# Channel attention over 384 x 384 x 384 in two passes: the opening of the second pass re-cut, two packed blocks stored together, 24-row reads up to then

## The chip, the cores and the metric

One core of a Trainium2 chip runs the whole kernel in one launch. The metric is the time of one execution on the device in microseconds (us), less is better. An execution can also be recorded by the hardware profiler; its page and its trace are what is read here. In a page PE is TensorE (matrix products), DVE VectorE, ACT ScalarE, POOL GpSimd and SP SyncE, which here only issues loads. "SPq" and "ACTq" are those engines' instruction queues, from which transfers (DMAs) are issued: loads from SP, stores from ACT.

## What is computed

```python
def reference(x, w1, w2):                 # x: 1 x 384 x 384 x 384, w1: 384 x 96, w2: 96 x 384, all bf16
    xf = x.reshape(B, H * W, C)
    gap = jnp.mean(xf, 1)                 # mean over all pixels, per channel
    gmp = jnp.amax(xf, 1)                 # maximum over all pixels, per channel
    h_a = gap @ w1
    h_a = h_a * (h_a > 0)
    h_m = gmp @ w1
    h_m = h_m * (h_m > 0)
    scale = sigmoid(h_a @ w2 + h_m @ w2)
    return x * scale[:, None, None, :]
```

The scale depends on every pixel, so `x` (113 MB) is read once for the mean and the maximum, and each element is multiplied and written after that. What doesn't stay on the chip in between has to be read a second time.

## The kernel before

The 147,456 pixels are cut into 1,152 rows for each of the 128 partitions. "A row" below is one pixel of 384 channels in every partition, 128 x 768 bytes = 98,304 bytes; a load of n rows moves n x 768 contiguous bytes for each partition.

**First pass.** SP loads blocks of rows; TensorE sums them (L260), VectorE keeps a running maximum in `acc`, 11 rows wide (L326). What can stay on the chip stays: 96 rows at the start of the buffer `body` (three slots of 31, 31 and 34 rows, at `body` rows 0, 31 and 62), 21 rows in `held`, 10 rows in PSUM, and seven packed blocks. A packed block is 32 rows in the space of 24 (`homes[i]`, `body` rows 96 + 24 i and on): three parts a, b and w of 8 rows, and a part d of 8 rows whose bytes are hidden in the others by `pack`. If a test finds values that the packing can't hold (`bad`), these blocks are read again at the very end; with this data they are not.

**Between the passes.** The maximum is folded, both branches go through `w1` and `w2`, and the scale lands in `scale_bc` (L418). The first rows of `held` (8, `refill`) and the 11 rows of `acc` are loaded in the meantime from SP (L402, L399).

**Second pass, opening** (L526 to L538). `put` multiplies pieces of a buffer in place on VectorE (L423) and has ACT store each (L432); `put_acc` does the same for `acc`. It begins with the first 6 rows of slot 0, then `acc`, the rest of slot 0, `held`, then slots 1 and 2. In between, `read(-1, 0)` has SP load the first of the rows that are needed again, into rows of `body` whose stores are done: SP waits in its own queue until the stores of just these rows have landed.

**Second pass, turns** (L546 to L564). `PLACES` lists, for each of the 28 turns, the first row of `body` and the number of rows that the turn's read goes to; `RING` = 96 rows, and after some packed stores also `body` rows from 96 up. A turn multiplies its rows on VectorE, has ACT store them (L477), has SP read into every place that is free by then (`read(turn, gone)`, L520), and then does one entry of `jobs`: `unpack(i, h)` restores half h of packed block i (eight instructions on VectorE, L455 and L460, and six copies on ACT, L474), `finish(i)` multiplies a restored block, 24 rows of `homes[i]` and 8 rows of `homes_d[i]`, the place where part d was restored to. Blocks 0 and 1 are also stored by `finish`, as is part d of block 2; the others are stored in the last three turns (`after`). `gone` tells `read` that the rows from 96 up may be used: it is set after turn 3, where block 0 is finished and stored, and place (96, 24) is the ninth. The three last stores (`leaving`) bring rows that were kept in PSUM, by way of `held` and `acc`.

Each engine takes its instructions in the order in which they are written; loads share one queue (q1 in the page) and stores another (q10), both over the same 16 DMA engines.

Of the kernel before, what the change touches and what calls it, by code (L numbers as in the profile page):

```python
# [32 lines left out]
RING = 96  # L33
G = 8
PACKED = 7
PSUM_ROWS = 8
LATE_ROWS = 8
BANK_ROWS = 2
# [14 lines left out]


PLACES = (
    ((0, 24), (24, 24), (48, 24), (72, 24)) * 2 + ((96, 24),)
    + ((0, 30), (30, 30), (60, 30), (90, 30)) * 4 + ((0, 30), (30, 30), (60, 26))
)
FIRST_READ = (8, 8, 8)
FILLS = 16  # L60
FIRST_STORES = ((1, 2, 3, 4, 4, 5, 6, 6), (9, 10, 12), (16, 18))
HELD_STORES = (6, 7)
ACC_STORES_AT = 3
TEST_SCALE = 0.031187
SUM_TAIL = 4
MM_ROWS = 4
# [3 lines left out]
def kernel(  # L70
# [22 lines left out]
    def rows_of(ap, block):  # L93
        first, n = block
        return ap[first * P:(first + n) * P, :].rearrange("(p n) c -> p n c", n=n)
# [8 lines left out]
    def take(n):  # L104
        nonlocal at
        at += n
        return at - n, n

    ps_block = take(PSUM_ROWS)
    beside = take(BANK_ROWS + A)  # L110
    packed_block = take(GP * PACKED)
    held_block = take(sum(LAST_HELD))
    stay = {s: take(sum(pieces)) for s, pieces in STAYING.items()}
# [28 lines left out]
    acc = consts.tile([P, A, C], BF16)  # L142
    nc.dynamic_dma_scratch_size = RING_BYTES
    nc.lookup_mloc("DynamicDMAScratchLoc").dims = [P, RING_BYTES]
    held = nc.alloc_sbuf_tensor_at("held", [P, HELD_ROWS, C], BF16, offset=RING_BYTES).ap()
    body = xpool.tile([P, RING + 3 * G * PACKED, C], BF16, name="body")
    slots = [body[:, SLOT * i:SLOT * i + stay[i][1], :] for i in range(NS)]
    spare = body[:, SLOT * NS, :]
    homes = [body[:, RING + 3 * G * i:RING + 3 * G * (i + 1), :] for i in range(PACKED)]
# [67 lines left out]
    for i in range(PACKED):  # L217
        first, d_at = 3 * G * i, 3 * G * PACKED + G * i
# [20 lines left out]
    for block, buf, pieces in parts_left:  # L239
        for j, m in enumerate(pieces):  # L240
            lo = sum(pieces[:j])
# [86 lines left out]
    def turn_over(out_, rows):  # L328

        for r in range(LATE_ROWS):  # L330
            for q in range(CQ):
                nc.tensor.transpose(  # L332
                    out=out_[:, r, q * P:(q + 1) * P], in_=rows[:, r, q * P:(q + 1) * P], identity=ident_bf
                )
# [11 lines left out]
    for st in steps:  # L346
# [8 lines left out]
        _, block, rows, lo, hi = st  # L355
# [9 lines left out]
        j = max(0, min(m, A - done))  # L365
# [55 lines left out]
    def multiply(dst, src):  # L421
        n = dst.shape[1]
        nc.vector.tensor_tensor(  # L423
            out=dst, in0=src, in1=scale_bc.unsqueeze(1).to_broadcast([P, n, C]), op=ALU.mult
        )

    def put(block, buf, pieces, lo=0):
        j = 0
        for m in pieces:
            rows = buf[:, j:j + m, :]  # L430
            multiply(rows, rows)
            nc.scalar.dma_start(out=rows_of(orr, block)[:, lo + j:lo + j + m, :], in_=rows)  # L432
            j += m

    def put_acc():
        for lo, hi in acc_pieces:
            multiply(acc[:, lo:hi, :], acc[:, lo:hi, :])
            nc.scalar.dma_start(out=acc_rows(orr, lo, hi), in_=acc[:, lo:hi, :])


    turns = len(PLACES)
    homes_d = [held[:, G * (i % 2):G * (i % 2 + 1), :] for i in (1, 0, 1)]
    homes_d += [homes[1][:, G * i:G * (i + 1), :] for i in range(3)] + [held[:, 0:G, :]]
    assert len(homes_d) == PACKED
    HG = G // 2
    m = held[:, 2 * G:2 * G + HG, :]
# [29 lines left out]
    def store(buf, block, lo):  # L476
        nc.scalar.dma_start(out=rows_of(orr, block)[:, lo:lo + buf.shape[1], :], in_=buf)  # L477

    d_at = 3 * G * PACKED

    def finish(i):

        for rows in (homes[i], homes_d[i]):
            multiply(rows, rows)
        if i < 2:
            store(homes[i], packed_block, 3 * G * i)
        if i < 3:
            store(homes_d[i], packed_block, d_at + G * i)


    jobs = [[(unpack, 0, 0)], [(unpack, 0, 1)], [(unpack, 1, 0)], [(finish, 0)], [(unpack, 1, 1)], [], [(finish, 1)]]
    jobs += [[(unpack, 2, 0)], [(unpack, 2, 1)], []]
    for i in range(3, PACKED):
        jobs += [[(unpack, i, 0)], [(finish, i - 1)], [(unpack, i, 1)]]
    jobs.append([])
    jobs.append([(finish, PACKED - 1)])

    after = [
        [(body[:, RING + 3 * G * 2:RING + 3 * G * 4, :], 3 * G * 2)],
        [(body[:, RING + 3 * G * 4:RING + 3 * G * 6, :], 3 * G * 4)],  # L500
        [(homes[1], d_at + 3 * G), (homes_d[6], d_at + 6 * G), (homes[6], 3 * G * 6)],
    ]

    order = []
# [2 lines left out]
    def read(last_turn, blocks_gone):  # L507

        if not again:
            return False  # L510
        k = len(PLACES) - len(again)
        lo, n = PLACES[k]
        if lo + n > RING + 3 * G * blocks_gone or max(turn_of_row[lo:lo + n]) > last_turn:
            return False
        turn_of_row[lo:lo + n] = [k] * n
        buf, b = body[:, lo:lo + n, :], again.pop(0)
        assert b[1] == n
        j = 0
        for m in FIRST_READ if k == 0 else (n,):
            nc.sync.dma_start(out=buf[:, j:j + m, :], in_=rows_of(xr, b)[:, j:j + m, :])  # L520
            j += m
        assert j == n
        order.append((b, buf))
        return True

    k = ACC_STORES_AT  # L526
    put(stay[0], slots[0], FIRST_STORES[0][:k])
    put_acc()
    j = sum(FIRST_STORES[0][:k])
    put(stay[0], slots[0][:, j:, :], FIRST_STORES[0][k:], j)  # L530
    put(held_block, held[:, LATE_ROWS:, :], HELD_STORES, LATE_ROWS)
    put(refill, held[:, 0:LATE_ROWS, :], (LATE_ROWS,))
    read(-1, 0)
    put(stay[1], slots[1], FIRST_STORES[1])
    read(-1, 0)
    put(stay[2], slots[2], FIRST_STORES[2])
    read(-1, 0)
    read(-1, 0)  # L538
    nc.vector.tensor_scalar(out=flag, in0=bad_ps, scalar1=0.5, scalar2=None, op0=ALU.is_gt)
# [1 line left out]
    assert len(jobs) <= turns - 3  # L541
    gone = 0

    leaving = [(held[:, G:G + PSUM_ROWS, :], ps_block), (acc[:, 0:LATE_ROWS, :], held_block)]
    leaving.append((acc[:, LATE_ROWS:LATE_ROWS + BANK_ROWS, :], beside))
    for turn in range(turns):  # L546
        b, buf = order.pop(0)
        multiply(buf, buf)
        if turn >= turns - len(after):
            for rows, lo in after[turn - turns + len(after)]:  # L550
                store(rows, packed_block, lo)
        store(buf, b, 0)
        while read(turn, gone):
            pass
        for job, *which in jobs.pop(0) if jobs else ():
            job(*which)
            gone = gone or job is finish
        if turn == turns - 3:
            to = leaving[1][0]
            nc.vector.tensor_copy(out=to.bitcast(U32), in_=late.bitcast(U32))  # L560
            turn_over(late, to)
            multiply(leaving[0][0], kept_ps[:, 0:PSUM_ROWS, :])
            multiply(leaving[2][0], kept_b)
            multiply(to, late)  # L564
# [40 lines left out]
```

## Time and profile before

| | us |
|---|---|
| three runs: median (lowest to highest) | 729.07 (729.03 to 729.39) |
| the profiled execution, its own time | 729.27 |
| its span in the page | 727.5 |
| VectorE busy | 565.0 (78%) |
| ScalarE busy | 349.5 (48%) |
| TensorE busy | 189.8 (26%) |
| HBM read / written | 192.14 MB / 113.25 MB, 420 GB/s over the span |

The span is what the profiler saw from the first instruction to the last; some 1.8 us of the execution lie around it. The page's second part cuts the span into 40 slices of 18.2 us, with a busy share in tenths for each engine and the bytes moved in each. A window gives the same for any stretch: start and end, length, busy time and number of instructions of PE, PEld (weight loads), DVE, ACT and POOL, the granted clock of TensorE, the share of DMA engines that were busy, and GB/s. A DMA share a little over 1 comes from packets whose records overlap. A line of waits reads "who <- whom: total us, times, longest". The chain of work that ended last is listed as start, duration, what. For a transfer the trace also has the time of its issue and of its landing, when the last of its bytes is told to have arrived, and the time that each packet (one partition's bytes) took.

The first pass ends near 273 us, the opening of the second runs from 278.0 to 305, its first turn starts at 306.6 and its last multiply ends at 680.8; the last store lands at 725.8.

### The profile page before, as it was taken

Reading aid. Unit: us, or ns where it says so; the run is one execution under the profiler, and the core shown is the slowest. Engines: PE = TensorE matmul, PEld = TensorE weight load, DVE = VectorE, ACT = ScalarE, POOL = GpSimd, SP = SyncE. Lnnn points to the kernel's source line nnn. Section 1 sums busy time; section 2 is a strip of 40 time slices with the busy share of each in tenths; the row PEclk is TensorE's granted clock in tenths of the full one; section 3 lists DMA queues with packets and bytes.
Section 4 is the critical chain, followed back from the end, with each engine's and each line's share of the span. In section 5 each row is a group of like instructions: output and inputs, shape, how many; then the busy total and the mean of one; then the engine's idle time right before and its main releaser. Section 6 shows DMA issues by size and latency. Waiting matters only on the chain.

```text
span 727.5 us, 3877 instructions
## 1 busy us (share of the span) xinstructions
PE 189.8 (26%) x1357; PEld 73.9 (10%) x1357; DVE 565.0 (78%) x440; ACT 349.5 (48%) x251; POOL 0.7 (0%) x6
## 2 busy tenths in 40 slices
PE   5767577885657461000000000000000000000000
PEld 1222222232222140000000000000000000000000
DVE  6799999999999998979969372989688894954200
ACT  6979999999999100058042703063443603000000
POOL 0000000000000000000000000000000000000000
PEclk9879877797897555555555555555555555555555
DMA  9999999999999979999999999999999999999997
GB/s 382 430 429 420 434 422 434 432 424 430 428 427 421 421 312 332 424 422 427 436 426 431 434 431 427 434 429 427 432 431 431 436 431 429 437 431 439 430 426 328
DMA packets 22563, 305.63 MB, mean 420 GB/s; under 512 B 2864, under 2 KB 3472, under 8 KB 9616
## 3 DMA queue, kind: packets, MB, share of 16 engines
q1 hardware_dynamic: 14048, 192.14, 62.3%
q10 hardware_dynamic: 8496, 113.25, 36.5%
q8 instruction: 10, 0.16, 0.1%
q14 instruction: 9, 0.07, 0.0%
HBM read 192.14 MB, written 113.25 MB: 420 GB/s over the span
## 4 chain that ended last, share of the span: by engine, by line
DMA 64%; DVE 26%; issue 2%; PE 1%; SPq 0%; ACT 0%; DVEq 0%; ACTq 0%
DMA body<-in_x_dram 47%; DMA out_dram<-body 17%; DVE body L423 13%; DVE acc L326 10%; DVE held L423 1%; PE words_ps L308 1%; DVE held L455 1%; PE bank_a L260 0%; DVE acc L423 0%; DVE acc L460 0%; DVE body L460 0%; DVE kept_ps L380 0%; DVE body L455 0%; DVE acc L455 0%; DVE acc L367 0%
## 5 line engine op out<-in xcount | busy, mean ns | idle before, releaser
L423 DVE TENSOR_TENSOR body<-body,scale_bc 128x11520 bf16<-128x11520 bf16 (+14 forms) x51 | 220.2, 4352 | 90.3 <-DMA body<-in_x_dram 87.5
L326 DVE TENSOR_TENSOR acc<-acc,body 128x2304 bf16<-128x2304 bf16 (+4 forms) x210 | 229.7, 1168 | 14.6 <-DMA body<-in_x_dram 14.5
L260 PE MATMUL bank_a<-body,small 128*1 128x512 bf16 (+2 forms) x849 | 92.2, 477 | 81.9 <-DMA body<-in_x_dram 81.9
L332 PE MATMUL words_ps<-ident_bf,acc 128*128 128x128 bf16 x24 | 2.7, 313 | 375.9 <-DVE acc L560 375.9
L288 ACT ACTIVATE held<-held 128x3072 uint8<-128x3072 uint8 (+1 forms) x35 | 82.1, 2346 | 1.1
L474 ACT COPY body<-body 128x1536 uint8<-128x1536 uint8 x20 | 29.5, 1477 | 93.5 <-DVE body L423 93.1
L287 ACT ACTIVATE held<-body,held 128x3072 uint8<-128x3072 int8 (+1 forms) x28 | 62.0, 2214 | 9.4 <-DMA body<-in_x_dram 9.0
L474 ACT COPY held<-body 128x1536 uint8<-128x1536 uint8 x8 | 11.8, 1476 | 100.8 <-DVE body L423 59.8
L474 ACT COPY body<-acc 128x1536 uint8<-128x1536 uint8 x34 | 49.6, 1475 | 8.0 <-DVE acc L460 7.6
L260 PEld LDWEIGHTS <-small 128*1 128x1 bf16 x891 | 30.4, 96 | 143.7 <-issue 123.2
L332 PEld LDWEIGHTS <-acc 128*128 128x128 bf16 x24 | 2.5, 147 | 376.3 <-DVE acc L560 376.3
L308 PE MATMUL words_ps<-body,scale_bc 128*128 128x512 fp8e4 (+1 forms) x126 | 39.4, 427 | 2.7 <-ACT body L315 2.7
L308 PE MATMUL words_ps<-body,w_sb 128*128 128x512 fp8e3 x84 | 27.2, 408 | 0.0
L308 PE MATMUL words_ps<-held,body 128*128 128x512 fp8e4 x84 | 25.5, 385 | 0.0
L314 ACT COPY body<-held 128x1536 uint8<-128x1536 uint8 x14 | 20.6, 1472 | 0.0
L474 ACT COPY acc<-body 128x1536 uint8<-128x1536 uint8 x14 | 20.5, 1468 | 0.0
L314 ACT COPY body<-body 128x1536 uint8<-128x1536 uint8 x14 | 20.5, 1463 | 0.0
L315 ACT ACTIVATE body<-words_ps 128x1536 uint16<-128x1536 f32 x14 | 20.2, 1442 | 0.0
L287 ACT ACTIVATE held<-held 128x3072 uint8<-128x3072 int8 x7 | 20.0, 2857 | 0.2
L326 DVE TENSOR_TENSOR acc<-acc,held 128x1920 bf16<-128x1920 bf16 (+4 forms) x18 | 17.5, 1012 | 0.1
L308 PE MATMUL words_ps<-body 128*128 128x512 fp8e3 x42 | 16.5, 394 | 0.0
L455 DVE TENSOR_SCALAR held<-held 128x1536 uint16<-128x1536 uint16 x28 | 15.7, 560 | 1.0
(71 smaller groups left out, 169.7 us busy)
## 6 DMA issues: line engine op xcount, KB each, us to landing
body<-in_x_dram SPq DMA_DIRECT2D x20, 2976.0 KB, 21.7
body<-in_x_dram SPq DMA_DIRECT2D x19, 2880.0 KB, 22.1
out_dram<-body ACTq DMA_DIRECT2D x18, 2880.0 KB, 26.2
body<-in_x_dram SPq DMA_DIRECT2D x14, 2304.0 KB, 16.6
out_dram<-body ACTq DMA_DIRECT2D x13, 2304.0 KB, 29.5
out_dram<-body ACTq DMA_DIRECT2D x2, 4608.0 KB, 42.1
held<-in_x_dram SPq DMA_DIRECT2D x8, 768.0 KB, 22.5
body<-in_x_dram SPq DMA_DIRECT2D x5, 960.0 KB, 15.3
```

The source lines that it names most:

```text
L260: nc.tensor.matmul(sum_ps[q * QP:q * QP + 1, 0:g * P], lhsT=ones_bf[:, 0:1], rhs=rows[:, k:k + g, q * P:(q + 1) * P], start=(done + k == 0 ...
L287: nc.scalar.activation(out=out_, in_=rows, func=ACT.Square, bias=test_bias, scale=TEST_SCALE)
L288: nc.scalar.activation(out=out_, in_=out_, func=ACT.Square, bias=minus4, accum_out=tests[:, k:k + 1],)
L308: nc.tensor.matmul(words[:, c:c + BANK], lhsT=weights[2 * r + k], rhs=high(part(i, r), dt)[:, half * n + c:half * n + c + BANK], start=(r ...
L314: nc.scalar.copy(out=high(part(i, r), U8)[:, span], in_=low(part(i, r + 2), U8)[:, span])
L315: nc.scalar.activation(out=part(i, 2).rearrange("p n c -> p (n c)").bitcast(U16)[:, span], in_=words, func=ACT.Copy, bias=32767.5,)
L326: nc.vector.tensor_tensor(out=out_, in0=in0, in1=in1, op=ALU.max)
L332: nc.tensor.transpose(out=out_[:, r, q * P:(q + 1) * P], in_=rows[:, r, q * P:(q + 1) * P], identity=ident_bf)
L423: nc.vector.tensor_tensor(out=dst, in0=src, in1=scale_bc.unsqueeze(1).to_broadcast([P, n, C]), op=ALU.mult)
L455: nc.vector.tensor_scalar(out=u16(dst), in0=u16(src), scalar1=s1, scalar2=s2, op0=op0, op1=op1)
L474: nc.scalar.copy(out=dst, in_=src)
```

## The change

- `PLACES`: three rounds of four places of 24 rows in place of two, then (96, 24), then three rounds of 30 and a last one of 30, 30, 30 and 20 rows: 29 turns and not 28, for the same 782 rows. The first read comes in two pieces (8, 16) and not three.
- The opening starts with the last 7 rows of slot 0 (3, 4), then `acc`, then all of `held`, then the other 24 rows of slot 0 (8 to 16, 16 to 24, 0 to 8). Before the second read come the first 17 rows of slot 1 (8, 9) and the first 10 of slot 2, and then the other 14 and 24 rows in one piece each.
- `finish` stores nothing for block 0. When block 1 is finished (turn 6), blocks 0 and 1 leave in one store of 48 rows and their parts d, now side by side in `held`, in one of 16. Part d of block 2 stays in `held` until the end. `gone` is set with block 1.
- Jobs for blocks 2 to 6 come later in the list; part d of block i is restored to another place (`homes_d`).
- The rows that were kept in PSUM leave by way of `body` rows 110 to 120 and not of `held` and `acc`; `late` still leaves from `acc`.

```diff
 PLACES = (
-    ((0, 24), (24, 24), (48, 24), (72, 24)) * 2 + ((96, 24),)
-    + ((0, 30), (30, 30), (60, 30), (90, 30)) * 4 + ((0, 30), (30, 30), (60, 26))
+    ((0, 24), (24, 24), (48, 24), (72, 24)) * 3 + ((96, 24),)
+    + ((0, 30), (30, 30), (60, 30), (90, 30)) * 3 + ((0, 30), (30, 30), (60, 30), (90, 20))
 )
-FIRST_READ = (8, 8, 8)
+FIRST_READ = (8, 16)
-FIRST_STORES = ((1, 2, 3, 4, 4, 5, 6, 6), (9, 10, 12), (16, 18))
+OPENING = (0, 24, (3, 4))
+FIRST_PLACE = ((0, 8, (8, 8)), (0, 0, (8,)))
+SECOND_PLACE = ((1, 0, (8, 9)), (2, 0, (10,)))
+OTHER_PLACES = ((1, 17, (14,)), (2, 10, (24,)))
...
-    homes_d = [held[:, G * (i % 2):G * (i % 2 + 1), :] for i in (1, 0, 1)]
-    homes_d += [homes[1][:, G * i:G * (i + 1), :] for i in range(3)] + [held[:, 0:G, :]]
+    homes_d = [held[:, G * (i % 2):G * (i % 2 + 1), :] for i in range(4)]
+    homes_d += [homes[1][:, G * i:G * (i + 1), :] for i in range(3)]
...
-        if i < 2:
-            store(homes[i], packed_block, 3 * G * i)
-        if i < 3:
-            store(homes_d[i], packed_block, d_at + G * i)
+        if i == 1:
+            store(body[:, RING:RING + 3 * G * 2, :], packed_block, 0)
+            store(held[:, 0:2 * G, :], packed_block, d_at)
...
-    jobs += [[(unpack, 2, 0)], [(unpack, 2, 1)], []]
+    jobs += [[], [], [], [(unpack, 2, 0)], [(unpack, 2, 1)]]
...
-        [(homes[1], d_at + 3 * G), (homes_d[6], d_at + 6 * G), (homes[6], 3 * G * 6)],
+        [(held[:, 0:2 * G, :], d_at + 2 * G), (homes[1], d_at + 4 * G), (homes[6], 3 * G * 6)],
...
-    k = ACC_STORES_AT
-    put(stay[0], slots[0], FIRST_STORES[0][:k])
+    def put_slot(i, lo, pieces):
+        put(stay[i], slots[i][:, lo:, :], pieces, lo)
+
+    put_slot(*OPENING)
     put_acc()
-    j = sum(FIRST_STORES[0][:k])
-    put(stay[0], slots[0][:, j:, :], FIRST_STORES[0][k:], j)
     put(held_block, held[:, LATE_ROWS:, :], HELD_STORES, LATE_ROWS)
     put(refill, held[:, 0:LATE_ROWS, :], (LATE_ROWS,))
+    for pieces in FIRST_PLACE:
+        put_slot(*pieces)
     read(-1, 0)
-    put(stay[1], slots[1], FIRST_STORES[1])
+    for pieces in SECOND_PLACE:
+        put_slot(*pieces)
     read(-1, 0)
-    put(stay[2], slots[2], FIRST_STORES[2])
+    for pieces in OTHER_PLACES:
+        put_slot(*pieces)
     read(-1, 0)
     read(-1, 0)
...
-    leaving = [(held[:, G:G + PSUM_ROWS, :], ps_block), (acc[:, 0:LATE_ROWS, :], held_block)]
-    leaving.append((acc[:, LATE_ROWS:LATE_ROWS + BANK_ROWS, :], beside))
+    j = PLACES[-1][0] + PLACES[-1][1]
+    leaving = [(body[:, j:j + PSUM_ROWS, :], ps_block), (acc[:, 0:LATE_ROWS, :], held_block)]
+    leaving.append((body[:, j + PSUM_ROWS:j + PSUM_ROWS + BANK_ROWS, :], beside))
...
-            gone = gone or job is finish
+            gone = gone or (job is finish and which[0] == 1)
```

More of the change, by code (lines that the diff above doesn't have):

```diff
@@ L55 @@
 PLACES = (
-    ((0, 24), (24, 24), (48, 24), (72, 24)) * 2 + ((96, 24),)
-    + ((0, 30), (30, 30), (60, 30), (90, 30)) * 4 + ((0, 30), (30, 30), (60, 26))
+    ((0, 24), (24, 24), (48, 24), (72, 24)) * 3 + ((96, 24),)
+    + ((0, 30), (30, 30), (60, 30), (90, 30)) * 3 + ((0, 30), (30, 30), (60, 30), (90, 20))
 )
-FIRST_READ = (8, 8, 8)
+FIRST_READ = (8, 16)
 FILLS = 16
-FIRST_STORES = ((1, 2, 3, 4, 4, 5, 6, 6), (9, 10, 12), (16, 18))
+OPENING = (0, 24, (3, 4))
+FIRST_PLACE = ((0, 8, (8, 8)), (0, 0, (8,)))
+SECOND_PLACE = ((1, 0, (8, 9)), (2, 0, (10,)))
+OTHER_PLACES = ((1, 17, (14,)), (2, 10, (24,)))
 HELD_STORES = (6, 7)
-ACC_STORES_AT = 3
 TEST_SCALE = 0.031187
@@ L542 @@
     gone = 0
-    leaving = [(held[:, G:G + PSUM_ROWS, :], ps_block), (acc[:, 0:LATE_ROWS, :], held_block)]
-    leaving.append((acc[:, LATE_ROWS:LATE_ROWS + BANK_ROWS, :], beside))
+    j = PLACES[-1][0] + PLACES[-1][1]
+    assert j + PSUM_ROWS + BANK_ROWS <= PLACES[-5][0] + PLACES[-5][1]
+    leaving = [(body[:, j:j + PSUM_ROWS, :], ps_block), (acc[:, 0:LATE_ROWS, :], held_block)]
+    leaving.append((body[:, j + PSUM_ROWS:j + PSUM_ROWS + BANK_ROWS, :], beside))
     for turn in range(turns):
```

## The prediction

> **What bounds the kernel now.** First the page's forty slices, then windows of the second pass, the waits, and the chain.
>
> ```profile
> DMA  9999999999999979999999999999999999999997
> GB/s 382 430 429 420 434 422 434 432 424 430 428 427 421 421 312 332 424 422 427 436 426 431 434 431 427 434 429 427 432 431 431 436 431 429 437 431 439 430 426 328
> ```
>
> The DMA engines are full in every slice but those around 255 to 291 us and the last. The windows cut the second pass finer (stretch, its length, five engines' busy time, clock, DMA share, GB/s):
>
> ```profile
> 280.00:286.00 6.00, 0.00 (x0) 0.00 (x0) 6.00 (x7) 0.00 (x0) 0.00 (x0) 0.50 0.95 370
> 286.00:290.00 4.00, 0.00 (x0) 0.00 (x0) 4.00 (x4) 0.00 (x0) 0.00 (x0) 0.50 1.01 339
> 290.00:295.00 5.00, 0.00 (x0) 0.00 (x0) 5.00 (x3) 0.00 (x0) 0.00 (x0) 0.50 1.01 411
> 295.00:306.00 11.00, 0.00 (x0) 0.00 (x0) 9.99 (x5) 0.00 (x0) 0.00 (x0) 0.50 1.03 424
> 314.00:322.00 8.00, 0.00 (x0) 0.00 (x0) 3.24 (x5) 7.18 (x5) 0.00 (x0) 0.50 1.00 399
> 330.00:700.00 370.00, 2.74 (x24) 2.48 (x24) 264.62 (x143) 110.20 (x77) 0.00 (x0) 0.50 1.01 431
> ```
>
> From 330 us to 700 the transfers run at 431 GB/s with a share of 1.01; VectorE (DVE) is busy for 265 of those 370 us. So the bytes set the end, and only what leaves the DMA engines idle or inefficient moves it. Waits say the same:
>
> ```profile
> SPq L520 <- DMA out_dram<-body: 361.7, 32, 23.6
> ...
> DVE body L423 <- DMA body<-in_x_dram: 87.5, 21, 13.5
> ```
>
> SP's queue waits 362 us for stores to land before it may read into their rows, and DVE waits 87.5 us for reads (13.5 at most). Neither costs anything while the other queue feeds the engines. The chain at the opening:
>
> ```profile
> 278.01 1.50 DVE body L423 x3
> 279.51 0.77 DVE acc L423
> 280.28 0.21 issue
> 280.49 1.35 DVE acc L423
> 281.85 5.34 DVE body L423 x5
> 287.19 4.41 DVE held L423 x3
> ```
>
> DVE starts at 278.01 when the scale is ready. The 0.21 us at 280.28 is the last row of `acc` landing (the trace: 280.21): the second `acc` multiply can't start earlier, whatever stands before it.
>
> **Prices.** At the end nothing but stores is queued, and landings in a row give their cost without sharing: 48 rows 10.88 us (685.23 to 696.11), 30 rows 6.81, 26 rows 5.91, 24 rows 5.46 and 5.45, 8 rows 1.85 and 1.87. That is 0.227 to 0.232 us a row (98,304 bytes), or 4.4 rows/us. I take 16 rows as 3.7 and 20 as 4.55.
>
> **Turns.** 9 places of 24 rows, 18 of 30 and one of 26 become 13, 15 and one of 20; rows stay 782. One way: before 9 x 5.455 + 18 x 6.81 + 5.91 = 177.6; after 13 x 5.455 + 15 x 6.81 + 4.55 = 177.6. The 29th turn costs one more store and read issue (0.34 us each on ACT's and SP's queues, idle there) and 0.07 us of DVE. Sum 0.
>
> **Packed stores.** Before, blocks 0 and 1 leave as 24 + 8 + 24 + 8, d of block 2 as 8, the rest of d and homes 1 and 6 at the end as 24 + 8 + 24: 4 x 5.455 + 4 x 1.86 = 29.3. After: 48 + 16, and 16 + 24 + 24: 10.88 + 2 x 3.7 + 10.9 = 29.2. So the merged store, the change's first words, saves 0.1 us at most. The Trainium skill ("DMA: Bandwidth & Descriptors", section "Anatomy of one DMA") puts about 2.0 us of fixed cost on each DMA beside bytes over 436 GB/s. Stores fall from 59 to 54, so an estimate by that page is 10 us off. The trace does not bear it out inside a queue: 8 rows follow the store ahead in 1.85 us, and their bytes alone make 1.80 at 436.
>
> **Opening.** Up to 281.85 nothing moves, since `acc` gates: 17 rows are multiplied before, 18 after. Then DVE gives a row per 0.21 us (from start to start 6 rows take 1.27 us, 7 rows 1.47, 8 rows 1.66), the engines take one per 0.23 to 0.24. Before: pieces 4, 4, 5, 6, 6; after: 6 and 7 of `held`, 8, and three of 8. By the trace's packets the slots' 13 old pieces (1 to 18 rows) cost 22.6 us and the 10 new ones 22.4: gain 0.2. The first read now waits for rows 0 to 8, stored last of slot 0. By rows: the `acc` pieces land at 284.7, then 6 + 7 + 32 rows at 0.235 follow: 295.3. It is issued then and not at 285.76, and the other three reads stand behind it on SP's queue. Until then only stores run, and I bound their rate by the store-only 370 GB/s of 280 to 286 and the 424 around 303 us. They serve 63 rows landed at 295.3 and some 1.5 on the way; before, the trace's packets from 279 us, when the `acc` loads end, to 295.3 sum to 60.5 rows, with the dip to 339 GB/s where reads begin inside it. That dip, (1 - 339/424) x 4 = 0.8 us, now comes 10 us later, so of the 4 rows ahead (0.9 us) 0.1 to 0.3 stays. Places 1 and 2 open earlier or alike: rows 31 to 48 are stored as 8 + 9 ahead of everything else of the slots, so the second read starts near 303 (before 306.83), while the first still runs; the queue of reads then doesn't run empty between the two, and part of the second dip (399 GB/s at 314 to 322: 0.6 us) may go. I take 0.3 of it. Gain of the opening: 0.2 to 1.0, taken as 0.6.
>
> By the Trainium skill ("Perfetto Trace Analysis", section "DMA Optimizations") smaller pieces let work start sooner, which speaks against a first piece of 3 rows in place of 1: multiplied at 278.7 and not 278.37, 0.35 us lost, the sum 728.9 and not 728.5. The row at 280.28 speaks against that: the next stores are gated by `acc` in both.
>
> **First read turn.** Pieces of 8 + 16 land some 13 us after 295.3 at half share, near 309; DVE is free for it at 306.5, so turn 0 starts 2 to 3 us late. What covers it: stores of 128 rows and two reads issued by 310 are 176 rows, 40 us of DMA from 280.5.
>
> **Turns 3 to 7.** Finish 0 no longer stores its 32 rows (7.3 us) and place (96, 24) opens at turn 7 and not 4 (24 rows of read-ahead). The ring is now 4 places of 24: 48 rows a turn, 10.9 us of DMA, against DVE's 4.9 + 5.2 (unpack) or 4.9 + 6.6 (finish). Four buffers make a loop of 43.7 us; one buffer's own way is 5.5 + 2 + 4.9 + 6.6 + 5.5 + 2 = 26.5, so over 17 us of work stays queued. The windows from 330 on show it: before turn 3 no packed store existed, and the share was 1.0. Cost 0; without the cover, 0.6 us in each of two finish turns.
>
> **The block at turn 6.** 64 rows (14.6 us) enter ACT's queue near 387 (the trace: finish 1 ends at 387.0), before the store of turn 7, for which the read of turn 11 waits, and behind it on SP all others. By my estimate 123 store rows are ahead then (11 left of turn 5, 24 of turn 6, the 64, turn 7's own 24) and 63 read rows (15 left of one, two whole): 186 x 0.227 = 42 us, so it is issued near 430 and lands near 443. Meanwhile the stores of turns 8 to 10, 72 rows, and the two reads (48) keep the engines busy to 457; turn 11's store comes at 448.5. Cover 8.5 us; cost 0.
>
> **Tail and edits at nothing.** `leaving` moves to `body` rows 110 to 120, so DVE waits between turns 26 and 27 for turn 24's store to land, and turns 27 and 28 and their stores stand behind it. Counted from the end, that store landed at 650.4 before and the read of the last turn but one at 659.1, so the wait is over before the next data come; and the last stores take 40 to 48 us from issue to landing, so 40 us are queued. Unpacks of blocks 2 to 6 come two to three turns later; their targets in `held` are free near 424 (99 store and 63 read rows after 387), the first copy could write at 421: 3 us at most, inside the wait for turn 11. Cost 0, or what DVE slips over 30 us at the end.
>
> **Sum.** Execution 729.27 (span 727.5 and 1.8 around it), 0.2 above the median 729.07. Off: 0.6 + 0.1 = 0.7: 728.5 in its own terms and 728.4 against the median.
>
> **Rivals.** (a) The dips go altogether: no restart of the read queue. Then 0.8 (286 to 290), 0.15 (290 to 295), 0.6 (314 to 322) and 0.4 of pieces and rows come off: 727.1. For it: reads follow each other after 303. Against: a first read from an empty queue remains. (b) The engines run dry after the 64-row block: if the read of turn 11 lands after 452 (443.5 plus the cover of 8.5), DVE has nothing to store. DVE's longest wait now is 13.5 us; less the cover, up to 5 us are lost, 2 to 5: 730.5 to 733.5, say 732. Against it: the 16 us of stores of turns 8 to 10. (c) The store-only opening runs at 370 to 295 us: (1 - 370/410) x 10 = 1.0 us lost: 729.4. (d) Each DMA pays a fixed time in its queue, about 10 us off, 719; the landings at the end speak against it.
>
> **How the numbers follow.** Forecast 0.62 (own range 727.9 to 729.2), (a) 0.20, (b) 0.11, (c) 0.05, (d) 0.02. A measurement of this kernel can tell 0.2% (1.46 us) from no change: 727.6 to 730.5. Faster is (a) and (d), 0.22; same is the forecast and (c), 0.67; slower (b), 0.11. The range 726.9 to 729.9 leaves out (b) and (d).
>
> **What would show it.** Right: GB/s of 400 or more from 283 to 295, the first L520 issue at 294 to 297, the dip after it, share 1.0 and 431 GB/s from 330 to 700, SP's issue gap before turn 11's read near 430. Wrong: any 5 us window in 350 to 460 with a share under 0.95, a first read later than 300, or a last store landing off 725.1 by over 1 us.

## The result and the profile after

The changed kernel takes 727.41 us (median of 10 executions, 727.13 to 728.70), the kernel before, run beside it, 729.07 (10 executions, 728.27 to 730.64). The ratio is 0.998 with an interval of 0.9972 to 0.9988: 0.9 to 2.0 us less, 1.66 by the medians. That is 0.23%, at the edge of the 0.2% that the prediction called tellable, and the interval reaches to both sides of it; by the prediction's own mark of 727.6 it is just on the side of faster, to which the prediction gave a chance of 0.22. The time lies inside the predicted range, 1.0 below the forecast of 728.4 and 0.5 below the likeliest case's own range. The profiled execution took 727.18 us with a span of 725.4, against 729.27 and 727.5.

The forty slices of the changed kernel, then its windows over the same stretches as before (stretch, length, busy time of five engines, clock, DMA share, GB/s):

```profile
DMA  9999999999999988999999999999999999999998
GB/s 382 429 427 423 432 425 435 426 432 427 426 428 422 421 330 347 399 425 437 425 438 424 434 434 428 425 433 428 431 437 428 429 436 432 432 430 442 426 427 362
```

```profile
280.00:286.00 6.00, 0.00 (x0) 0.00 (x0) 6.00 (x6) 0.00 (x0) 0.00 (x0) 0.50 0.99 397
286.00:290.00 4.00, 0.00 (x0) 0.00 (x0) 4.00 (x4) 0.00 (x0) 0.00 (x0) 0.50 1.02 425
290.00:295.00 5.00, 0.00 (x0) 0.00 (x0) 5.00 (x4) 0.00 (x0) 0.00 (x0) 0.50 1.02 419
295.00:306.00 11.00, 0.00 (x0) 0.00 (x0) 9.46 (x4) 0.00 (x0) 0.00 (x0) 0.50 1.03 389
314.00:322.00 8.00, 0.00 (x0) 0.00 (x0) 7.83 (x8) 6.67 (x6) 0.00 (x0) 0.50 1.02 429
```

The dip of the opening has moved. From 286 to 290 us the transfers ran at 339 GB/s before and run at 425 now; from 295 to 306, where the first read now starts, 424 became 389; from 314 to 322, 399 became 429. The last slice moves more (328 to 362): everything ends earlier. The middle is as it was:

```profile
330.00:700.00 370.00, 2.74 (x24) 2.48 (x24) 263.29 (x141) 107.25 (x75) 0.00 (x0) 0.50 1.01 431
```

The two waits that the prediction quoted, and the chain through the opening (start, duration, what):

```profile
SPq L522 <- DMA out_dram<-body: 358.8, 28, 29.2
...
DVE body L426 <- DMA body<-in_x_dram: 87.5, 25, 11.9
```

```profile
279.30 0.23 DVE acc L426
279.53 0.76 issue
280.29 1.35 DVE acc L426
281.64 4.41 DVE held L426 x3
286.05 5.02 DVE body L426 x3
...
291.08 3.92 DMA out_dram<-body
...
295.06 0.33 SPq L522
...
295.49 12.44 DMA body<-in_x_dram
```

SP waits as long for stores as before and DVE as long for reads (87.5 us in sum, 11.9 at most instead of 13.5). The chain lists the second `acc` multiply at 280.29 (280.49 before). It waits for no landing, in either kernel: the 0.76 us called issue are the first `acc` multiply, which runs from 279.22 to 280.37, and the last row of `acc` had landed at 279.46. Before, it landed at 280.21, and the first `acc` multiply ran from 279.42 to 280.58. Then come `held` and slot 0, whose last store lands at 295.00; the first read is issued at 295.06. The prediction said 295.3.

**Where 2.1 us of span went.** 0.33 lies ahead of the second pass (its first multiply starts at 277.68 and not 278.01; the change touches nothing before it), 1.52 between that multiply and the last landing (447.79 became 446.27), and 0.24 between the last landing and the end (1.68 became 1.44). This last part is a matter of count and not of speed: the loads and stores share eight semaphores, at the end SP waits for these one after the other at some 0.07 us each, and the last store happens to use one that leaves 10 such waits behind it and not 13. Over the kernels below, the time behind the last landing goes from 1.31 us with 8 waits to 1.86 with 15. To place the 1.52 I take, for a stretch, its length less the bytes of its packets at 432 GB/s, the rate at which the last stores run. This "lost time" is:

| us lost | first 52 us after the first multiply | the next 388 us | from there to the last landing |
|---|---|---|---|
| before | 4.18 | 0.73 | 2.32 |
| after | 3.67 | 0.68 | 1.23 |

The sums differ by 1.65 and not by 1.52, so such a figure is good to some 0.15 us. The opening gained 0.5, the middle nothing, and the end 1.1. At the end only stores are queued. Three windows there, of the kernel before and then of the changed one:

```profile
722.00:723.00 1.00, 0.00 (x0) 0.00 (x0) 0.00 (x0) 0.00 (x0) 0.00 (x0) 0.50 0.95 387
723.00:724.00 1.00, 0.00 (x0) 0.00 (x0) 0.00 (x0) 0.00 (x0) 0.00 (x0) 0.50 0.47 183
724.00:726.00 2.00, 0.00 (x0) 0.00 (x0) 0.00 (x0) 0.00 (x0) 0.00 (x0) 0.50 0.06 25
```

```profile
722.00:723.00 1.00, 0.00 (x0) 0.00 (x0) 0.00 (x0) 0.00 (x0) 0.00 (x0) 0.50 0.62 249
723.00:724.00 1.00, 0.00 (x0) 0.00 (x0) 0.00 (x0) 0.00 (x0) 0.00 (x0) 0.50 0.16 58
724.00:726.00 2.00, 0.00 (x0) 0.00 (x0) 0.00 (x0) 0.00 (x0) 0.00 (x0) 0.50 0.00 0
```

The share falls over two to three microseconds because the 16 DMA engines don't finish together. The trace has sixteen completion marks for each transfer, which I take as one of each engine. Of the last store, the first came at 723.07 and the last at 725.80 before, with a single one 0.86 us behind the next; now they come at 722.46 and 723.95. The share of 0.06 over 724 to 726 is mostly that one engine's tail, and the kernel ends with it.

### The profile page after: what moved, and what is told of

It is laid out like the page before. It is cut to its first block, busy times and chain, and to the rows that moved or that the text cites. A ratio compares the mean times of both kernels' runs of the same rounds, so it can differ in the third digit from the quotient of the medians.

```text
span 725.4 us, 3863 instructions
## 1 busy us (share of the span) xinstructions
PE 188.9 (26%) x1357; PEld 73.4 (10%) x1357; DVE 565.1 (78%) x438; ACT 349.6 (48%) x251; POOL 0.7 (0%) x6
## 4 chain that ended last, share of the span: by engine, by line
DMA 71%; DVE 20%; issue 2%; PE 0%; ACT 0%; SPq 0%; ACTq 0%; DVEq 0%
DMA body<-in_x_dram 52%; DMA out_dram<-body 19%; DVE acc L329 11%; DVE body L426 7%; DVE held L426 1%; DVE held L458 0%; DVE kept_ps L383 0%; DVE acc L426 0%; ACT held L477 0%; DVE acc L463 0%; DVE acc L370 0%; PE bank_a L263 0%; DVE body L458 0%; SPq L360 0%; PE bank_a L420 0%
## 5 line engine op out<-in xcount | busy, mean ns | idle before, releaser
L426 DVE TENSOR_TENSOR body<-body,scale_bc 128x9216 bf16<-128x9216 bf16 (+8 forms) x49 | 220.1, 4523 | 88.7 <-DMA body<-in_x_dram 87.5
L329 DVE TENSOR_TENSOR acc<-acc,body 128x2304 bf16<-128x2304 bf16 (+4 forms) x210 | 229.7, 1167 | 14.1 <-DMA body<-in_x_dram 14.1
L477 ACT COPY held<-acc 128x1536 uint8<-128x1536 uint8 x8 | 11.8, 1475 | 10.1 <-DVE acc L463 10.1
```

The lines of the kernel that those rows point to most:

```text
L329: nc.vector.tensor_tensor(out=out_, in0=in0, in1=in1, op=ALU.max)
L426: nc.vector.tensor_tensor(out=dst, in0=src, in1=scale_bc.unsqueeze(1).to_broadcast([P, n, C]), op=ALU.mult)
L477: nc.scalar.copy(out=dst, in_=src)
```

## Experiments

Each kernel is compared with the kernel before, run in between on the same chip (729.15 for the first four, 729.24 for the next four, 729.06 for the last four; 29 to 35 executions each; each four on another chip, so a few tenths between groups can't be told apart). The last five columns come from one profiled execution each: its time, lost time in the three stretches above, and the time between the first and the last completion mark of the last store ("spread"). That execution need not be a typical one: for e2_block, e8_hold and e12_long it is the slowest, for e6_places the fastest.

| kernel | median us (range, executions) | ratio and interval | profiled | opening | middle | end | spread |
| --- | --- | --- | --- | --- | --- | --- | --- |
| before | 729.07 (728.27 to 730.64, 10) | 1 | 729.27 | 4.18 | 0.73 | 2.32 | 2.7 |
| after | 727.41 (727.13 to 728.70, 10) | 0.998 [0.9972, 0.9988] | 727.18 | 3.67 | 0.68 | 1.23 | 1.5 |
| e1_open | 729.17 (727.56 to 730.02, 12) | 0.9994 [0.9985, 1.0003] | 729.34 | 3.62 | 0.83 | 2.93 | 3.7 |
| e2_block | 728.06 (727.83 to 728.65, 11) | 0.9985 [0.9976, 0.9993] | 728.65 | 4.11 | 0.14 | 1.87 | 2.0 |
| e3_unmerged | 727.31 (727.03 to 727.98, 9) | 0.9975 [0.9965, 0.9984] | 727.17 | 3.63 | 0.02 | 1.72 | 1.5 |
| e4_early | 728.35 (727.65 to 730.53, 11) | 0.9995 [0.9986, 1.0004] | 728.27 | 3.64 | 0.84 | 1.89 | 2.6 |
| e5_split | 729.06 (727.90 to 736.43, 12) | 1.0002 [0.9983, 1.0022] | 728.92 | 3.64 | 1.15 | 2.11 | 2.5 |
| e6_places | 728.32 (727.81 to 729.18, 12) | 0.9987 [0.9979, 0.9996] | 727.81 | 3.92 | 0.22 | 1.63 | 1.6 |
| e7_defer | 727.55 (727.43 to 727.74, 12) | 0.9978 [0.9970, 0.9987] | 727.45 | 3.99 | -0.14 | 1.77 | 1.8 |
| e8_hold | 737.16 (736.22 to 737.28, 5) | 1.0105 [1.0089, 1.0121] | 737.28 |  |  |  |  |
| e9_both | 727.37 (727.03 to 728.29, 11) | 0.9981 [0.9972, 0.9990] | 727.37 | 3.48 | 0.08 | 1.60 | 1.7 |
| e10_short | 728.06 (727.70 to 728.76, 11) | 0.9988 [0.9980, 0.9997] | 727.92 | 4.02 | -0.14 | 1.78 | 1.7 |
| e11_both_unmerged | 728.16 (727.59 to 738.01, 12) | 1.0003 [0.9980, 1.0025] | 730.49 | 3.74 | 0.54 | 4.20 | 4.4 |
| e12_long | 727.72 (727.22 to 728.87, 11) | 0.9985 [0.9976, 0.9993] | 728.87 | 3.84 | 0.84 | 2.25 | 2.4 |

### Which part of the change

**e1_open: the new opening alone.** The kernel before, with only the lines of the opening changed.

```diff
-FIRST_READ = (8, 8, 8)
+FIRST_READ = (8, 16)
+OPENING = (0, 24, (3, 4))
...
```

> The kernel before with the new opening alone (order and sizes of the opening's stores, first read in 8 + 16). Theory O, the opening holds the gain: 0.8 to 1.6 us under the kernel before, first L520 read issued near 295 us, 390 to 425 GB/s from 280 to 295. Theory B, the rest of the plan (turns, packed stores, the last stores) holds it: 0 to 0.5 us under the kernel before, with the same look of the opening.

The opening does in this kernel what it does in the whole change: 3.62 us lost and not 4.18, and the dip moves, as these windows of it show.

```profile
286.00:290.00 4.00, 0.00 (x0) 0.00 (x0) 4.00 (x4) 0.00 (x0) 0.00 (x0) 0.50 1.01 422
...
295.00:306.00 11.00, 0.00 (x0) 0.00 (x0) 9.90 (x5) 0.00 (x0) 0.00 (x0) 0.50 1.01 383
```

But the kernel is not measurably faster (0.9994, an interval that holds 1), as theory B had said. In the profiled execution the end ate the gain: its engines finish 3.7 us apart.

```profile
722.00:723.00 1.00, 0.00 (x0) 0.00 (x0) 0.00 (x0) 0.00 (x0) 0.00 (x0) 0.50 0.70 286
723.00:724.00 1.00, 0.00 (x0) 0.00 (x0) 0.00 (x0) 0.00 (x0) 0.00 (x0) 0.50 0.39 157
724.00:726.00 2.00, 0.00 (x0) 0.00 (x0) 0.00 (x0) 0.00 (x0) 0.00 (x0) 0.50 0.12 48
```

**e2_block: everything but the opening.** The changed kernel with the old `FIRST_READ` and `FIRST_STORES`.

```diff
-FIRST_READ = (8, 16)
+FIRST_READ = (8, 8, 8)
...
+FIRST_STORES = ((1, 2, 3, 4, 4, 5, 6, 6), (9, 10, 12), (16, 18))
```

> The changed kernel with the old opening. Theory O: 0 to 0.5 us under the kernel before, with the 339 GB/s dip at 286 to 290 us back. Theory B: 1.0 to 1.6 us under it, last stores landing within 1.5 us of one another per engine, although the dip is back.

728.06: 1.1 us come from what the prediction had priced at 0.1, and the opening adds some 0.65 to it (728.06 to 727.41, with intervals that overlap). By the profiles 0.32 of this lies behind the last landing (1.76 us here, with 14 semaphore waits, against 1.44). The old dip is back (320 GB/s from 286 to 290).

**e3_unmerged: the block in four stores.** The changed kernel, but blocks 0 and 1 leave at turn 6 as 24 + 24 + 8 + 8 rows.

```diff
-            store(body[:, RING:RING + 3 * G * 2, :], packed_block, 0)
-            store(held[:, 0:2 * G, :], packed_block, d_at)
+            for i in range(2):
+                store(homes[i], packed_block, 3 * G * i)
+            for i in range(2):
+                store(homes_d[i], packed_block, d_at + G * i)
```

> The changed kernel with blocks 0 and 1 stored at turn 6 as 24 + 24 + 8 + 8 in place of 48 + 16. Theories O and B without the merge: as the changed kernel, within 0.2 us (the prediction's price of the merge is 0.1). If the number of DMAs counts by itself (a third theory, D: some 0.3 us for each of the five DMAs fewer), 0.6 us above the changed kernel.

727.31 beside 727.41: joining the stores, which the change is named for, gives nothing that can be measured, and the 0.1 is what lies behind the last landing (1.31 us against 1.44). With it falls the theory that a store less saves a fixed time (theory D), by which it would have been 0.6 more.

**e4_early: slot 0 first, then `held`.** The first read can then be issued at 287.03 and not 295.06.

```diff
-    put(held_block, held[:, LATE_ROWS:, :], HELD_STORES, LATE_ROWS)
-    put(refill, held[:, 0:LATE_ROWS, :], (LATE_ROWS,))
-    for pieces in FIRST_PLACE:
+    for pieces in FIRST_PLACE[::-1]:
         put_slot(*pieces)
     read(-1, 0)
+    put(held_block, held[:, LATE_ROWS:, :], HELD_STORES, LATE_ROWS)
+    put(refill, held[:, 0:LATE_ROWS, :], (LATE_ROWS,))
...
```

> The changed kernel with slot 0 stored whole before the held rows, so that the first read starts early again, near 289 us, with the new piece sizes. Theory O in the form of the prediction (the gain is that reads start late and only once): 0.4 to 0.9 us above the changed kernel, the dip back at 289 to 292 us and a second one near 315. If only the sizes and the order up to there count, or theory B: within 0.3 us of the changed kernel.

The dip moves with the read and keeps its size, some 0.9 us in both kernels when counted as the prediction counts it. A second dip near 315 does not come back:

```profile
286.00:290.00 4.00, 0.00 (x0) 0.00 (x0) 4.00 (x4) 0.00 (x0) 0.00 (x0) 0.50 1.00 323
295.00:306.00 11.00, 0.00 (x0) 0.00 (x0) 9.79 (x4) 0.00 (x0) 0.00 (x0) 0.50 1.02 419
...
314.00:322.00 8.00, 0.00 (x0) 0.00 (x0) 2.40 (x4) 7.17 (x5) 0.00 (x0) 0.50 0.99 426
```

3.64 us are lost in this opening and 3.67 in the change's own, so the late first read is not what the opening's gain comes from. What both have and the kernel before lacks is full rate from 314 to 322 us. The timed runs (728.35, with the interval 0.9986 to 1.0004) put it 0.9 behind the changed kernel by the medians, as much as theory O had said; but the profile shows this at the end (1.89 against 1.23, the engines 2.6 us apart), not in the opening.

**e6_places: the new `PLACES` alone.** The kernel before with the 29 turns.

```diff
-    ((0, 24), (24, 24), (48, 24), (72, 24)) * 2 + ((96, 24),)
+    ((0, 24), (24, 24), (48, 24), (72, 24)) * 3 + ((96, 24),)
...
```

> The kernel before with the new PLACES alone (29 turns, three rounds of 24 rows): blocks 0 and 1 are stored as before, the opening is the old one. Theory R: goes by the number of empty stretches of the read queue after 330 us in its trace, 0.3 to 0.5 us for each one fewer than before's three; as reads are evenly sized up to turn 12, one or two should go: 0.4 to 1.0 us under the kernel before. Theory B: within 0.3 us of the kernel before.

728.32: 0.9 less than before, though the queue of reads still stops three times (for 10.9 us at 383.6, 10.5 at 424.1 and 6.7 at 489.7), as in the kernel before (10.1, 10.3 and 6.2). The theory named R in these texts, that each such stop costs 0.3 to 0.5 us, doesn't fit that.

**e7_defer: blocks 0 and 1 deferred, with the old places and opening.** The kernel before with the new `homes_d`, one store of both blocks, `gone` set with block 1, and what hangs on that.

```diff
...
+        if i == 1:
+            store(body[:, RING:RING + 3 * G * 2, :], packed_block, 0)
+            store(held[:, 0:2 * G, :], packed_block, d_at)
...
-    jobs += [[(unpack, 2, 0)], [(unpack, 2, 1)], []]
+    jobs += [[], [], [(unpack, 2, 0)], [(unpack, 2, 1)]]
...
+    j = 90
...
```

> The kernel before with the old PLACES and old opening, but blocks 0 and 1 deferred and stored together at turn 6, part d of block 2 kept to the end, and the PSUM rows leaving by way of body rows 90 to 100. Theory B: 0.8 to 1.2 us under the kernel before. Theory R: by the empty stretches that its trace shows, 0.3 to 0.5 us for each fewer than three; if there are still three, within 0.3 us of the kernel before.

727.55 in twelve executions that lie within 0.31 us: the deferral alone gives as much as the whole change. In this kernel no read runs for 23.7 us from 385.5 and then no store for 9.9, and the middle loses nothing (-0.14); DVE does nothing at all from 407 to 420, with the transfers at 442 GB/s:

```profile
386.00:407.00 21.00, 0.00 (x0) 0.00 (x0) 6.03 (x2) 0.00 (x0) 0.00 (x0) 0.50 1.00 429
407.00:420.00 13.00, 0.00 (x0) 0.00 (x0) 0.00 (x0) 0.00 (x0) 0.00 (x0) 0.50 1.03 442
420.00:430.00 10.00, 0.00 (x0) 0.00 (x0) 7.83 (x2) 0.00 (x0) 0.00 (x0) 0.50 0.99 426
```

**e9_both: e7_defer with the new opening** (the edits of e7_defer and e1_open together).

> The e7 kernel (old PLACES, blocks 0 and 1 deferred and stored together) with the new opening as well. If the opening's gain and the deferral's add: 726.9 to 727.2 us, 0.3 to 0.6 under e7 and the changed kernel. If the new opening gives nothing that lasts (as alone): 727.4 to 727.7 us.

727.37, no measurable addition to e7_defer, though its opening loses 0.5 us less (3.48 against 3.99). The profiles show where most of that went: from the first multiply to the last landing e9_both takes 445.98 us and e7_defer 446.38, but behind it stand 12 semaphore waits and not 8 (1.59 us against 1.31). The parts don't add up: places alone 0.9, deferral alone 1.7, both 1.1, the opening alone nothing by the medians and 0.4 by the ratio (with an interval from a loss of 0.2 to a gain of 1.1), 0.65 on one kernel and 0.2 on another, all three 1.66. Each of these is good to some 0.6.

**e5_split: the block taken apart.** The changed kernel, with the parts d stored at turn 6, block 0's home at turn 7 and block 1's at turn 9; `gone` is then set with block 0's.

```diff
-            store(body[:, RING:RING + 3 * G * 2, :], packed_block, 0)
...
+    def send(i):
+        store(homes[i], packed_block, 3 * G * i)
...
-    jobs += [[], [], [], [(unpack, 2, 0)], [(unpack, 2, 1)]]
+    jobs += [[(send, 0)], [], [(send, 1)], [(unpack, 2, 0)], [(unpack, 2, 1)]]
...
```

> The changed kernel with the 64-row block taken apart: the 16 rows of parts d leave at turn 6, home 0 (24 rows) at turn 7 and home 1 at turn 9. Theory R (each stretch in which the queue of reads stands empty and starts again costs the slowest DMA engine some 0.3 to 0.5 us; before has three of them after 330 us, the changed kernel one, near 424): the empty stretch near 424 us shrinks or goes, time 0 to 0.5 us under the changed kernel. Theory B (deferring and joining the packed stores is itself the gain): 0.3 to 1 us above the changed kernel.

The gain is gone (1.0002). The window from 450 to 510 us of this kernel and then of the changed one:

```profile
450.00:510.00 60.00, 0.00 (x0) 0.00 (x0) 42.08 (x30) 22.09 (x17) 0.00 (x0) 0.50 1.00 424
```

```profile
450.00:510.00 60.00, 0.00 (x0) 0.00 (x0) 51.39 (x40) 32.27 (x23) 0.00 (x0) 0.50 1.01 430
```

The share is 1.00 and 1.01, so nothing runs dry; about the same occupied time moves 424 and not 430 GB/s, 0.8 us in 60. Some packets take far longer than usual here (a packet of 24 rows usually takes 686 ns): nine in ten of the long ones take 80 to 570 ns more.

### Is it the stops of the reads?

The excess of such long packets (those over 60 ns beyond the usual for their size, from 330 to 720 us, summed over the 16 engines) comes to 12.4 us in the kernel before, 14.1 in e1_open, 14.6 in e4_early, 19.2 in e5_split, and 1.1 to 3.9 in e7_defer, e3_unmerged, e6_places and e2_block. Often they come just after the reads start again. Theory S took that up: a short stop of the reads ends in such packets when they start again and so costs some tenths of a microsecond, a long one does not. Three kernels make or lengthen stops, by having SP wait for a turn's multiply (a one-element load into `small` that nothing uses is added for it).

**e8_hold: three long holds in the part with 30-row turns.** Added to the changed kernel:

```diff
+HOLD_UNTIL = (16, 20, 24)
...
+        if turn in HOLD_UNTIL:
+            nc.vector.memset(small[0:1, 15:16], 0.0)
+            nc.sync.dma_start(out=small[0:1, 15:16], in_=w1[0:1, 0:1])
-        while read(turn, gone):
+        while not any(t - 3 <= turn < t for t in HOLD_UNTIL) and read(turn, gone):
```

> The changed kernel with reads held back three times in the later, even part (the queue of SP waits for the multiplies of turns 16, 20 and 24 and a one-element load), so that the queue of reads stands empty three times more while stores go on. Bytes, turns and stores are the same. Theory R: 0.9 to 1.5 us above the changed kernel, each restart showing as a stretch under 425 GB/s or as a later last store. If empty stretches cost nothing while stores flow: within 0.3 us of the changed kernel.

It didn't test that: the holds, some 12 to 16 us each, outlast the stores that are queued, and the engines idle.

```profile
560.00:580.00 20.00, 0.00 (x0) 0.00 (x0) 19.79 (x13) 4.72 (x4) 0.00 (x0) 0.50 0.91 370
```

Three holds cost 8 us over the kernel before and some 10 over the changed one. This is what running dry looks like and costs: the share falls below 1.

**e10_short: three holds of about 4 us in e7_defer**, at 518, 562 and 604 us.

```diff
+HOLD_UNTIL, HOLD = (15, 18, 21), 2
...
+        while not any(t - HOLD <= turn <= t for t in HOLD_UNTIL) and read(turn, gone):
...
```

> The e7 kernel with reads held back three times by some 7 to 8 us (SP waits for the end of the jobs of turns 15, 18 and 21 and a one-element load), so that the read queue stands empty for some 1 to 3 us three times, too briefly for the store queue to run dry. Theory S (a short stop of the reads beside running stores costs, since the packets around the restart take 150 to 500 ns longer on a few of the 16 engines, and an engine that has lost time doesn't get it back): 0.8 to 1.5 us above e7, with such packets after each restart and a spread of several tenths between single executions. If stops cost nothing: within 0.2 us of e7, as tight as e7.

No long packets follow (1.2 us in all), the middle loses as little as without the holds (-0.14), and the windows over two of them show full rate:

```profile
555.00:575.00 20.00, 0.00 (x0) 0.00 (x0) 18.83 (x13) 3.45 (x3) 0.00 (x0) 0.50 1.00 432
600.00:620.00 20.00, 0.00 (x0) 0.00 (x0) 15.86 (x13) 7.24 (x6) 0.00 (x0) 0.50 1.02 438
```

The median is 0.5 above e7_defer's, between what the two theories said. By the profiles none of it is the stops: from the first multiply to the last landing both kernels take 446.38 us, and 0.37 lies behind it (1.68 against 1.31), since the three one-element loads use semaphores too and SP goes through 13 waits and not 8. So these stops of the reads beside running stores did not delay the last landing, and S falls.

**e12_long: the one stop of the changed kernel made longer**, from 11.4 to 15.9 us (the reads of turns 11 and 12 wait for turn 10's unpack).

```diff
+HOLD_UNTIL, HOLD = (10,), 3
...
```

> The changed kernel with its one stop of the reads made longer: the reads of turns 11 and 12 wait for turn 10's unpack, some 4 us more, so that the read queue is empty for about 12 us and not 8. Theory S (short stops cost, long ones, in which all engines finish their reads, do not): 0 to 0.4 us under the changed kernel, no long packets after the restart, single executions closer together. If the length of a stop is what costs: 0.3 us or more above the changed kernel.

727.72, 0.3 above the changed kernel and no better; the long packets are still there (15.0 us, half of it from 460 to 465), though the profiled execution is the slowest of the eleven. S, which said that they would go, fails here too. The 0.3 is just what was named for a stop whose length costs; the intervals of the two kernels overlap, so this isn't shown.

**e11_both_unmerged: e9_both with the four stores of e3_unmerged.**

> As e9, with blocks 0 and 1 stored as 24 + 24 + 8 + 8 at turn 6. The merge itself counts (against the third experiment): 0.3 us or more above e9. It doesn't: within 0.2 us of e9.

Inconclusive: 0.9980 to 1.0025. By the medians it is 0.8 above e9_both, the sign that was named for a merge that counts; e3_unmerged, which has the same four stores and is as fast as the changed kernel, speaks against that. The profiled execution took 730.49 with one engine some 3 us late at the end (4.4 us between first and last), another one 738. In its trace the marks of a store drift apart steadily, from 3.1 us at 496 to 5.4 at 621, as if an engine ran slower all the while; in the changed kernel they stay 1.1 apart from 526 to 648. What made these executions late was not found.

## Why the prediction was right, and which step was mis-sized

- **What bounds the kernel**: right. Rate 431 GB/s and share 1.01 from 330 to 700 as before, and DVE can idle (e7_defer) or SP's reads stop (e10_short) without cost as long as the stores last.
- **Opening**: right in place; the size came out right in sum, but by other terms. First read issued at 295.06 (said 295.3), the second at 301.69 (303), turn 0's multiply at 308.05, 1.5 later than before (said 2 to 3); 416 GB/s from 283 to 286, then 425 and 419 to 295 (400 or more), the dip behind it at 296 to 298, and the second one gone (399 became 429 at 314 to 322; the prediction took half of it). 0.5 less is lost (said 0.6). The second dip alone makes an estimated (1 - 399/429) x 8 = 0.56 us of this, while the first keeps its size, of which the prediction had a part go; that the sum fits is in part luck. Rival (c), a thin rate while only stores run, fell at the 425. The prediction's reading of the row at 280.28 was wrong: the last row of `acc` lands at 280.21, but DVE is busy with the first `acc` multiply until 280.58, so nothing waits for that landing. From the first multiply to the second of `acc` pass 2.48 us before, with 11 rows multiplied between, and 2.61 now, with 12. (The Trainium skill, "Perfetto Trace Analysis", section "DMA Optimizations", says that splitting DMAs into smaller chunks may let some start sooner. The trace agrees on the start: the first store is issued 0.39 us after the first multiply begins with one row, 0.80 us with three. It shows no gain from it, since the opening with three rows loses 0.5 less.) Rival (a) named almost the measured time (727.1) but not by its mechanism: the dip of the first read stays, and e4_early shows that it goes where the read goes.
- **Packed stores**: right. Lone stores cost their rows: 48 in 10.89 us (said 10.88; its largest price a row, 0.232 us, should read 0.234, from 1.87 for 8 rows), 16 in 3.66 (3.7), 20 in 4.57 (4.55); e3_unmerged shows no worth of the merge. Rival (d), a fixed time for each DMA, fell with it. The Trainium skill ("DMA: Bandwidth & Descriptors", section "Anatomy of one DMA") gives its some 2 us fixed for each DMA for DMAs issued from GpSimd, a condition that the prediction left out; here they are issued from SP and ACT. By that figure an estimate for the two stores that e3_unmerged has more would be 4 us; it measured 0.1 less, so in a queue that is never empty the figure doesn't add to the time.
- **No dry spell**: right, and rival (b) fell. Turn 11's read is issued at 429.97 (said 430) and lands at 445.69 (443); its store follows at 450.70, inside the cover. One sign that the prediction gave against itself did come in, a window of 5 us with a share under 0.95: 0.88 from 405 to 410. The window ahead of it has 1.09 (400 to 405), and the two together 0.98. A window counts a packet whole where it starts, and the store of 48 rows, with packets of 1.36 us, was running then, so this is no dry spell. e8_hold shows what (b) would have looked like.
- **Turns 3 to 7, the block at turn 6, tail: the mis-sized step.** "Cost 0" was weighed only against what could go wrong: the prediction asked what covers the later stores and the later place and never what these edits could gain. Together they are worth 1.1 us (e2_block, interval 0.5 to 1.7), and the deferral without the new places 1.6 (e7_defer, 0.9 to 2.2). So of the 1.66 us measured, the prediction's 0.7 accounts for the opening's 0.5 alone; that the time still fell into its range, which also held no change at all, is in part luck. The sign that it gave itself, "a last store landing off 725.1 by over 1 us", came in: 723.95.

In the profiled pair that gain is not where these edits are, near 400 us, but at the end, where the last completion mark is 1.9 us earlier and the first 0.6. Another 0.24 is the three semaphore waits fewer behind it, which no term of the prediction had. The sum of the prediction treats the engines as one pipe of 432 GB/s. They are 16 pipes, which share a transfer's 128 packets, and the kernel ends with the slowest. Over the profiled executions the time from the first multiply to the last landing follows that spread: 446.0 to 446.4 us at spreads of 1.5 to 1.8 (e9_both, e3_unmerged, the changed kernel, e7_defer, e10_short, e6_places), 446.8 at 2.0 (e2_block), 447.0 to 447.6 at 2.4 to 2.6 (e4_early, e5_split, e12_long), 447.8 at 2.7 (before), 448.06 at 3.7 (e1_open), 449.08 at 4.4 (e11_both_unmerged). In the last 40 us, stores alone, each landing follows the one ahead by the time of its packets, and the spread stays as it is (2.72 to 2.77 us before, 1.47 to 1.51 now).

The completion marks also tell when the engines fall apart. Before, the sixteen marks of a store are 1.2 to 1.3 us apart from 316 to 381, 0.5 to 2.5 from 387 to 504, 3.9 at 513, and then 4.4 to 4.5 for every store from 528 to 650. In the changed kernel they are 0.3 apart from 324 to 430, 1.0 at 437, just after the reads start again at 429.97, 0.6 to 0.7 up to 497, and 1.1 from 526 to 648. In e3_unmerged they are 0.4 at 498, 0.8 at 512, and 1.1 from 526 on. So in these three most of the lag comes up between some 385 and 525 us, the stretch in which the reads stop and start again, and the even turns behind it neither add to it nor make it up. (While reads run too, an engine that is behind with stores may be ahead with reads, so these numbers change once more when the reads end.) The steps go with long packets: before, 4.1 of its 12.4 us of them lie from 500 to 520; e3_unmerged has three in all, 0.8 us of them at 506 and 513 and 0.4 at 653, and its spread goes from 1.1 to 1.5 between the stores that land at 648 and 662.

**What stays open.** Why packets are long in these stretches was not settled, nor why they leave so different spreads: the changed kernel has 11.7 us of them, nearly as much as before, and a spread of 1.5, and e7_defer has 1.1 us and 1.8. That the number of stores and the stops of the reads by themselves are the cause found no support; that the order of stores and reads in 380 to 510 us decides it is only what e2_block, e5_split, e6_places and e7_defer suggest together. Spreads are from one execution of each kernel, and the medians of ten move by some tenths.

## What to carry to other kernels

Where the transfers run at full rate from end to end, price an edit of the schedule on both sides of zero: moving stores by 10 to 30 us changed this kernel by 1 to 2 us with no idle time to show for it. Read the last windows by engine: the spread between the first and the last completion mark (1.5 to 4.4 us here) is time that no average rate shows. Where tenths count, compare kernels up to the last landing: what follows it (1.3 to 1.9 us here) changes with the number of transfers alone. Joining stores in a queue that is never empty was worth nothing measurable, and try the parts of a change singly before adding them up, since here they didn't add.

## What was not expected of the hardware

- The 16 completion marks of the last store lie 1.5 to 4.4 us apart (e8_hold left out), in kernels that differ only in the order and sizes of some stores and reads.
- A read that starts from an empty queue beside running stores takes the rate to 281 GB/s for 2 us (296 to 298 in the changed kernel); when reads stopped for some 4 us and started again in e10_short, nothing was lost.
- A packet's time is linear in its size: 121 to 125 ns for 4 rows, 234 for 8, 686 for 24, 855 for 30, 1364 for 48 (about 8 ns and 28.2 ns a row of 768 bytes); in mixed stretches some take 60 to 550 ns more.
- At most eight transfers were open at once, loads and stores together. This is the program's doing and not a queue's: they share eight semaphores, and an issue waits for the transfer before it on its own (landings at 682.92 and 693.81, issues on the same two semaphores at 682.94 and 693.83 in the changed kernel).
- From the last landing to the end of the span pass 1.3 to 1.9 us: SP goes through the 8 to 15 semaphore waits that are left, some 0.07 us each, and 0.8 us follow.
